# Gated mix of attention and token MLP: the tail of the output projection as half-row products, the o split on GpSimd, and where the max tiles stand

## The chip, the cores and the metric

The kernel runs on one core of one Trainium2 chip. The metric is device time in microseconds of one execution: before the change a median of 1803.75 us over three runs (1803.69 to 1805.62). One execution was profiled; it took 1802.82 us, and its span from the first to the last instruction is 1801.0 us.

The core has five engines with a queue each: TensorE (PE, whose weight loads the profile lists as PEld), VectorE (DVE), ScalarE (ACT), GpSimd (POOL) and SyncE (SP), which here issues all DMAs. Matmuls write to PSUM, of which there are eight banks of 128 x 512 words.

## The reference

`x` is 2048 x 640. Two branches are computed from it and mixed row by row by a gate.

```python
q = (x @ wq).reshape(B, S, 32, 20).transpose(0, 2, 1, 3)   # 32 heads of 20
k, v = x @ wk, x @ wv                                      # one head for all
p = softmax(einsum("bhqd,bkd->bhqk", q, k) * 20 ** -0.5)
a = einsum("bhqk,bkd->bhqd", p, v).transpose(0, 2, 1, 3).reshape(B, S, 640) @ wo
h = layernorm(x)                                           # over the 640 channels
u = gelu(einsum("bsd,sf->bdf", h, w1) + b1)                # over the tokens, F = 1728
b = (einsum("bdf,fs->bds", u, w2) + b2).transpose(0, 2, 1)
out = g * a + (1 - g) * b                                  # g = sigmoid(x . gate_w)
```

Everything is float32.

## The kernel before

**Precision.** A float32 operand is split into a high part, rounded to the type fp32r, and a low part, the rest. A product is then three products in fp32r: high x high, low x high, high x low. The names `oh` and `ol`, `wo_hi` and `wo_lo`, `w2h` and `w2l` are such pairs.

**Units and phases.** Attention is cut into 32 units (`NU`): four heads by 512 queries. A unit has 16 key blocks of 128 keys. The loop at L696 runs over phases `k`, one for each key block of each unit, 513 in all. Phase k issues, in one list for TensorE:

- four score products s (L443, 62 rows by 512 columns), two for key block k - 1 and two for k, all on one half of the rows of TensorE's array: rows 0 to 63 in even phases, 64 to 127 in odd ones (`b = k % 2`). ScalarE takes the exp of each into a tile p (L446);
- four max tiles ms (L284, while there are any): scores of a later unit, whose row maxima VectorE takes (L287) and which later go into the exp's argument;
- up to 16 half-row products with 320 columns of the rest of the work, called fs: first the first MLP layer (L626), then the second (L530), then the output projection (L577). They use the other half of the rows, so that a product of either half can run beside one of the other. They accumulate in the one bank of the pool `ps_g`;
- at the end the four o products of key block k - 1 (L470, `pv_mm`), with 128 rows by 32 columns each.

`beside` (L669) merges two lists, a lane for each row half, by adding up estimated times (`X_US` 0.232 for a product of 512 columns, `F_US` 0.147 for one of 320). In the lane of s there are three max tiles, in the lane of fs one (L702). The order on TensorE and VectorE is the program's own (L695, a manual schedule); ScalarE, GpSimd and SyncE are ordered by the framework's scheduler.

**The flag.** Products on both row halves accumulate in the same bank in turns, one half per phase. So that they don't overlap, `signal` (L454) puts a tiny memset on VectorE behind the last product of a lane, and the first product of the other half (`other_tile`, L449) waits for it.

**How long a phase's list of fs is.** `batches` (L635) spreads the steps of a tile over pairs of phases. First layer: 9 or 10 steps in a phase; second layer: 8 to 11; output projection of row tiles 0 to 11: 7 or 8 up to phase 463, and 15 from 464 to 499 (the long phases). The max tiles end with phase 487; then `spare[0]` is set (L708) and s takes its banks in turns from `ps_m` and `ps_s`, three banks each.

**End of a unit.** After its last o product VectorE transposes the sums (`ot`, L479). The list `later` then holds the steps that follow, one popped in each phase (L710): nothing; `scale` (reciprocal on VectorE L482, multiply on GpSimd L483); `back` (transpose on VectorE, L486); `store` (`oh` on ScalarE L489, `ol` on GpSimd L491, and eight DMAs to the scratch `o_scr`, L495). Once `spare[0]` is set, all four are popped in one phase, and the multiply and `ol` are on VectorE. That concerns units 30 and 31.

**The last four row tiles** (12 to 15) need unit 31, which ends last. From phase 500 (`k_tail`) their o rows of all but the last four heads (560 of 640 rows) are loaded, and phases 502 to 509 compute a part each (a row tile's 320 columns): 15 whole-row products in one bank (L577 through `last_parts`, L722), behind the phase's lanes. VectorE adds the part to the MLP branch (L585) in `spare_row`. After the loop, oh and ol of unit 31 are multiplied with the last four heads' rows of `wo` (L744), added (L745) and stored, one DMA for each row tile.

Of the kernel before, what the change touches and what calls it, by code (L numbers as in the profile page):

```python
# [9 lines left out]
F32 = mybir.dt.float32  # L10
# [27 lines left out]
def mix_kernel(ctx: ExitStack, tc: tile.TileContext, A_x, A_wq, A_wk, A_wv, A_wo,  # L38
# [5 lines left out]
    def f32(ap):  # L44
        return ap.bitcast(F32)
# [390 lines left out]
    def qk(u, pr, b):  # L436
        n, kb = units[u]
        if kb == 4 and pr == 0 and b == 0:
            new_q(n + 1)
        q = qtiles[n]  # L440
        odd_s[0] ^= 1
        s = ps_m.tile([P, NB], F32, name="ms") if spare[0] and odd_s[0] else ps_s.tile([P, NB], F32, name="s")
        nc.tensor.matmul(s, kst[64 * b:64 * b + 62, kb * P:(kb + 1) * P], q[64 * b:64 * b + 62, pr, :],  # L443
                         start=True, stop=True)
        p = pp_pool.tile([P, NB], F32, name="p")
        nc.scalar.activation(p, s, AF.Exp, scale=SCALE)  # L446
        ptiles[u, 2 * pr + b] = p
# [16 lines left out]
    def pv_mm(u):  # L464
        n, kb = units[u]
        if kb == 0:
            otile[0] = ps_o.tile([P, NB], F32, name="o")
        o = otile[0]
        for hh in range(4):
            nc.tensor.matmul(o[32 * hh:32 * hh + 32, :], v_sb[:, kb, :], ptiles.pop((u, hh)),  # L470
                             start=(kb == 0), stop=(kb == NS - 1), skip_group_check=True)
        if kb == NS - 1:
            qb, g = divmod(n, NQ)
            ot = ev.tile([P, NB // 32, 32], F32, name="ot")
            rl = ev.tile([P, NB // 32], F32, name="rl")
            on = ev.tile([P, NB], F32, name="on")
            oh = ev.tile([P, NB], F32R, name="oh")
            ol = ev.tile([P, NB], F32R, name="ol")
            nc.vector.transpose(ot.rearrange("p c e -> p (c e)"), o)  # L479

            def scale():
                nc.vector.reciprocal(rl, ot[:, :, DH])  # L482
                (nc.vector if spare[0] else nc.gpsimd).tensor_mul(ot, ot, rl[:, :, None].to_broadcast([P, NB // 32, 32]))  # L483

            def back():
                nc.vector.transpose(on, ot.rearrange("p c e -> p (c e)"))  # L486

            def store():
                nc.scalar.activation(oh, on, AF.Copy)  # L489
                osplit[:] = [oh, ol]  # L490
                (nc.vector if spare[0] else nc.gpsimd).tensor_sub(ol, on, f32(oh))  # L491
# [53 lines left out]
    def a_jobs(st, part=None):  # L545
        hold = {}
        rows = D if part is None else (H - 4) * DH
        kr = [min(P, rows - c * P) for c in range(DC)]

        def load():  # L550
            oT, yt = oTs[st % 2], yts[st % 2]
            cols = slice(st * P, (st + 1) * P)
            nf = rows // P
            for j in range(2):
                nc.sync.dma_start(out=f32(oT[:, j, :nf]),
                                  in_=o_scr[j, :nf * P, cols].rearrange("(c p) s -> p c s", p=P))
                if nf < DC:
                    nc.sync.dma_start(out=f32(oT[:kr[nf], j, nf]), in_=o_scr[j, nf * P:rows, cols])
            nc.sync.dma_start(out=yt, in_=y_scr[st * P:(st + 1) * P, :])
            hold["o"], hold["y"] = oT, yt  # L560
            if part is None:
                hold["a"] = pools["fin"].tile([P, D], F32, name="yo")
            else:
                hold["a"] = part[st] = spare_row(st)

        halves = [(0, 1) if r > 64 else (0,) for r in kr] if part is None else [(None,)] * DC
        total = 3 * sum(len(h) for h in halves)

        def mm(c, k, d, half):
            if not hold.get("n"):  # L570
                hold["p"], hold["n"] = (ps_m.tile([P, NB], F32, name="ms") if part is not None and d
                                        else ps_g.tile([P, NB], F32, name="g")), 0
# [3 lines left out]
            r = slice(0, kr[c]) if half is None else slice(64 * half, min(kr[c], 64 * half + 64))  # L576
            other_tile(half, nc.tensor.matmul(hold["p"][:, :HD2], o[r, c, :], w[r, c, d * HD2:(d + 1) * HD2],  # L577
                             start=(hold["n"] == 1), stop=(hold["n"] == total)))

        def done(d):  # L580
            sl = slice(d * HD2, (d + 1) * HD2)
            at, yt = hold["a"], hold["y"]
            hold["n"] = 0
            if spare[0]:
                nc.vector.scalar_tensor_tensor(at[:, sl], hold["p"][:, :HD2], g_col[:, st:st + 1], yt[:, sl],  # L585
                                               op0=ALU.mult, op1=ALU.add)
# [3 lines left out]
            if part is None and d == 1:  # L590
                nc.sync.dma_start(out=y_out[st * P:(st + 1) * P, :], in_=at)

        return load, [([[lambda h=h, c=c, k=k, d=d: mm(c, k, d, h) for h in halves[c]]
                        for c in range(DC) for k in range(3)],
                       lambda d=d: done(d)) for d in range(2)]
# [91 lines left out]
    def lane_f(ms, fs):  # L687
        return [(F_US, f) for f in fs] + [(0.0, signal)] + [(X_US, y) for y in ms]

    parts = {}  # L690
    tail = [a_jobs(st, parts) for st in range(NS - 4, NS)]
    last_parts = [(i, p) for i, (load, ps) in enumerate(tail) for p in ps]
    steps, rest = [], []
    w1_upto(4 * PRO + 4)
    with tc.manual_schedule(engines={mybir.EngineType.PE, mybir.EngineType.DVE}):  # L695
        for k in range(len(units) + 1):  # L696
# [2 lines left out]
            if not b:  # L699
                steps, rest = seq[k // 2] if k // 2 < len(seq) else ([], [])  # L700
            fs = [f[1 - b] for f in steps if b or len(f) > 1]
            ms = [[f for f in (ms_next(x) for _ in range(c)) if f] for x, c in ((b, 3), (1 - b, 1))]  # L702
            lanes = [None, None]
            lanes[b] = lane_x(ss, ms[0])
            lanes[1 - b] = lane_f(ms[1], fs)
            beside(*lanes, b)
            ms_done()
            spare[0] = len(row_max) == NU  # L708
            pop_chain()
            for _ in range(4 if spare[0] else 1):  # L710
                f = later.pop(0) if later else None
                if f:
                    f()
            if b:
                for f in rest:
                    f()
            j = k - k_tail
            if j == 0:
                w_last = last_wo()
                tail[0][0]()  # L720
                tail[1][0]()
            if 2 <= j < 2 + len(last_parts):  # L722
                i, (st_steps, done) = last_parts[j - 2]
                for f in st_steps:
                    f[0]()
                done()
                if j % 2 and i + 2 < len(tail):
                    tail[i + 2][0]()
            if k:
                pv_mm(k - 1)  # L730
                n, kb = units[k - 1]
                if kb == 7 and n + 1 < NU:
                    store_max(n + 1)
    for f in later[1:]:
        f()
    oh, ol = osplit
    for i in range(4):
        st = NS - 4 + i
        at = pools["fin"].tile([P, D], F32, name="yo")
        for d in range(2):  # L740
            sl = slice(d * HD2, (d + 1) * HD2)
            acc = ps_m.tile([P, NB], F32, name="ms")
            for k, (o, w) in enumerate(((oh, w_last[0]), (ol, w_last[0]), (oh, w_last[1]))):
                nc.tensor.matmul(acc[:, :HD2], o[:, i * P:(i + 1) * P], w[:, sl], start=(k == 0), stop=(k == 2))  # L744
            nc.vector.scalar_tensor_tensor(at[:, sl], acc[:, :HD2], g_col[:, st:st + 1], parts[st][:, sl],  # L745
                                           op0=ALU.mult, op1=ALU.add)
# [22 lines left out]
```

## Time and profile before

| what | value |
| --- | --- |
| median of three runs | 1803.75 us |
| profiled execution | 1802.82 us, span 1801.0 us |
| mean granted TensorE clock | 0.993 |
| first phase with o products to the last | 215.3 to 1785.7 us |
| long phases with max tiles (464 to 487) | from about 1600 to 1687 us |
| loads and parts of the last four row tiles | about 1737 to 1780 us |
| L446, exp on ScalarE | 1999 x 601 ns on s, 49 more on ms banks |
| L287, reduce on VectorE | 2048 x 683 ns |
| L489, `oh` on ScalarE | 32 x 632 ns; idle before it 22.6 us, for `on` |
| L491, `ol` on GpSimd | 30 x 1274 ns |
| from the last o product's end to the end of the span | 1787.3 to 1801.0 us |

How to read it: the profile gives for each group of instructions the busy time, the mean of one, and the idle time just before them with what ended it. A timeline lists instructions in order of time, merged where they follow each other: start, length, engine, line, operation, output<-input, shape, count, and in brackets the idle time before and its releaser. A row of a window gives, for a stretch of time, the busy time and count of each engine, then the granted clock, the share of the DMA engines and GB/s. An L470 group of eight records is the end of a phase.

### The profile page before, as it was taken

Reading aid. Unit: us, or ns where it says so; the run is one execution under the profiler, and the core shown is the slowest. Engines: PE = TensorE matmul, PEld = TensorE weight load, DVE = VectorE, ACT = ScalarE, POOL = GpSimd, SP = SyncE. Lnnn points to the kernel's source line nnn. Section 1 sums busy time; section 2 is a strip of 40 time slices with the busy share of each in tenths; the row PEclk is TensorE's granted clock in tenths of the full one; section 3 lists DMA queues with packets and bytes.
Section 4 is the critical chain, followed back from the end, with each engine's and each line's share of the span. In section 5 each row is a group of like instructions: output and inputs, shape, how many; then the busy total and the mean of one; then the engine's idle time right before and its main releaser. Section 6 shows DMA issues by size and latency. Waiting matters only on the chain.

```text
span 1801.0 us, 38745 instructions
## 1 busy us (share of the span) xinstructions
PE 1767.1 (98%) x14805; PEld 1141.4 (63%) x14805; DVE 1488.5 (83%) x3052; ACT 1211.6 (67%) x2360; POOL 441.9 (25%) x428
## 2 busy tenths in 40 slices
PE   7989999999999999999999999999999999999998
PEld 5779766666666666566666666666666666566654
DVE  7759999898999898988888888888888888887412
ACT  3334477777777777777777777777777777776653
POOL 6336532323232323142111111111111110111100
PEclk9999999999999999999999999999999999999999
DMA  6555422222222221222211111121111110233321
GB/s 198 158 159 138 106 53 60 66 60 61 66 66 66 66 66 43 73 85 72 65 45 53 58 58 50 54 58 58 58 58 58 48 47 24 63 110 107 98 87 50
DMA packets 155677, 133.66 MB, mean 74 GB/s; under 512 B 18103, under 2 KB 119892, under 8 KB 155492
## 3 DMA queue, kind: packets, MB, share of 16 engines
q1 hardware_dynamic: 155492, 131.18, 25.3%
q8 instruction: 117, 1.92, 0.5%
q14 instruction: 68, 0.56, 0.1%
HBM read 98.50 MB, written 31.13 MB: 72 GB/s over the span
## 4 chain that ended last, share of the span: by engine, by line
PE 91%; DVE 4%; DMA 2%; ACT 1%; issue 1%; POOL 1%; SPq 0%; DVEq 0%; POOLq 0%; ACTq 0%
PE o L470 29%; PE ms L284 17%; PE s L443 17%; PE g L530 11%; PE g L626 7%; PE g L577 4%; PE pp L180 3%; PE pu L391 2%; DVE mp L287 2%; DMA xt<-in_A_x_dram 1%; PE ms L443 1%; PE ms L577 1%; POOL wq_lo L117 0%; POOL slot L156 0%; PE ms L304 0%
## 5 line engine op out<-in xcount | busy, mean ns | idle before, releaser
L287 DVE TENSOR_REDUCE mp<-ms 128x1 f32<-128x512 f32 x2048 | 1279.2, 683 | 172.3 <-PE ms L284 166.4
L446 ACT ACTIVATE p<-s 128x512 f32<-128x512 f32 x1999 | 1047.5, 601 | 366.5 <-PE s L443 351.5
L284 PE MATMUL ms<-kst,qmx 60*128 60x512 f32 x2048 | 848.2, 423 | 4.0 <-DVE mp L287 2.4
L443 PE MATMUL s<-qst,kst 62*128 62x512 f32 x1999 | 745.4, 406 | 1.6 <-issue 1.1
L470 PE MATMUL o<-p,v_sb 128*32 128x512 f32 x4096 | 562.2, 605 | 0.5 <-ACT p L446 0.5
L284 PEld LDWEIGHTS ms<-kst,qmx 60*128 60x128 f32 x2048 | 378.5, 185 | 223.6 <-DVE flag L456 179.4
L443 PEld LDWEIGHTS s<-qst,kst 62*128 62x128 f32 x1999 | 372.1, 186 | 12.6 <-ACT p L446 8.6
L626 PE MATMUL g<-slot,wh 64*128 64x320 f32 x1152 | 282.0, 320 | 0.0
L626 PEld LDWEIGHTS g<-slot,wh 64*128 64x128 f32 x1152 | 191.3, 185 | 54.3 <-DVE flag L456 41.6
L530 PE MATMUL g<-slot,w2h 64*128 64x320 f32 x864 | 214.2, 321 | 0.0
L530 PE MATMUL g<-u,w2h 64*128 64x320 f32 x864 | 214.0, 321 | 0.0
L626 PE MATMUL g<-slot,wl 64*128 64x320 f32 x576 | 180.4, 313 | 0.0
L470 PEld LDWEIGHTS o<-p,v_sb 128*32 128x32 f32 x4096 | 94.4, 108 | 135.3 <-issue 124.1
L530 PEld LDWEIGHTS g<-slot,w2h 64*128 64x128 f32 x864 | 142.8, 184 | 53.7 <-DVE mp L287 28.5
L483 POOL TENSOR_TENSOR ot<-ot,rl 128x512 f32<-128x512 f32 x30 | 31.5, 1050 | 565.9 <-DVE rl L482 563.0
L530 PEld LDWEIGHTS g<-u,w2h 64*128 64x128 f32 x864 | 142.7, 184 | 42.2 <-DVE flag L456 26.8
L338 POOL TENSOR_TENSOR wl<-wr,wh 128x512 fp32r<-128x512 f32 x112 | 149.5, 1339 | 43.9 <-ACT wh L335 36.5
L577 PE MATMUL g<-slot 64*128 64x320 f32 (+1 forms) x780 | 134.1, 319 | 2.5 <-DVE yo L585 2.4
L577 PEld LDWEIGHTS g<-slot 64*128 64x128 f32 (+1 forms) x780 | 116.3, 188 | 28.5 <-DVE flag L456 10.1
L530 PE MATMUL g<-u,w2l 64*128 64x320 f32 x432 | 132.0, 306 | 0.0
L530 PE MATMUL g<-slot,w2l 64*128 64x320 f32 x432 | 132.0, 306 | 0.0
L337 POOL CAST wh<-wr 128x512 fp32r<-128x512 f32 x72 | 44.0, 610 | 293.2 <-PE g L626 293.2
(122 smaller groups left out, 1552.6 us busy)
## 6 DMA issues: line engine op xcount, KB each, us to landing
wr<-in_B_w_dram SPq DMA_DIRECT2D x104, 256.0 KB
qmx<-q_scr SPq DMA_DIRECT2D x192, 80.0 KB
qst<-q_scr SPq DMA_DIRECT2D x192, 80.0 KB
slot<-o_scr SPq DMA_DIRECT2D x24, 320.0 KB
w2r<-in_B_w_dram SPq DMA_DIRECT2D x16, 448.0 KB
w2r<-in_B_w_dram SPq DMA_DIRECT2D x16, 384.0 KB
xt<-in_A_x_dram SPq DMA_DIRECT2D x16, 320.0 KB
q_scr<-qh SPq DMA_DIRECT2D x20, 256.0 KB
```

Of the source, the lines that this page charges most:

```text
L180: nc.tensor.matmul(pp, w[:, c, :], t[c], start=(n == 0), stop=(n == len(pairs) * DC - 1))
L284: nc.tensor.matmul(ms, qmax[n][64 * b:64 * b + 60, pr, qt * P:(qt + 1) * P], kst[64 * b:64 * b + 60, kq * NB:(kq + 1) * NB], start=True, s ...
L287: nc.vector.tensor_reduce(mtiles[n][:, c, kq:kq + 1], ms, axis=AX.X, op=ALU.max)
L337: nc.gpsimd.tensor_copy(wh, wr)
L338: nc.gpsimd.tensor_sub(wl, wr, f32(wh))
L391: nc.tensor.matmul(pu[r][:, :HD2], w[rows, c, :], h[rows, st, :], start=(st == 0 and k == 0), stop=(st == NS - 1 and k == 2))
L443: nc.tensor.matmul(s, kst[64 * b:64 * b + 62, kb * P:(kb + 1) * P], q[64 * b:64 * b + 62, pr, :], start=True, stop=True)
L446: nc.scalar.activation(p, s, AF.Exp, scale=SCALE)
L470: nc.tensor.matmul(o[32 * hh:32 * hh + 32, :], v_sb[:, kb, :], ptiles.pop((u, hh)), start=(kb == 0), stop=(kb == NS - 1), skip_group_check ...
L530: other_tile(half, nc.tensor.matmul(hold["p"][:, :HD2], w[r, fc % FH, :], u[d][r, fc, :], start=(hold["n"] == 1), stop=(hold["n"] == 6 * F ...
L577: other_tile(half, nc.tensor.matmul(hold["p"][:, :HD2], o[r, c, :], w[r, c, d * HD2:(d + 1) * HD2], start=(hold["n"] == 1), stop=(hold["n" ...
L626: other_tile(half, nc.tensor.matmul(hold["p"][:, :HD2], w[r, st % HS, :], h[d][r, st, :], start=(hold["n"] == 1), stop=(hold["n"] == 6 * NS)))
```

## The change

1. **The o split.** `store` becomes two steps, `high` and `low`. `high` takes `oh` on GpSimd, except for the last unit (ScalarE). `low` takes `ol` on GpSimd, except for the last unit (VectorE), and issues the stores. In spare phases two steps are popped instead of four.
2. **Max tiles.** In phases with 12 or more fs, all four max tiles are in the lane of s (`(b, 4), (1 - b, 0)`).
3. **The last parts.** From phase 502 the parts of row tiles 12 to 15 are half-row products in both lanes: `tail_job` makes 30 for rows 0 to 63 and 24 for rows 64 to 127 of each row tile, with an accumulator of its own for each row half and column half (one in `ps_g`, three in `ps_m`), so that no flag is needed. `tail_take` gives them out, 8 or 7 behind the s of one lane and 13 or 16 in the other. VectorE adds each accumulator on its own, four in place of two additions for a row tile. Row tile st + 2 is loaded when st's four are done.
4. **s tiles.** From phase 501 s uses only its own three banks (`not loaded`).
5. **The end.** The output goes through p tiles (twelve buffers) in place of `yo` (two), one DMA for each half row tile.

```diff
-        s = ps_m.tile([P, NB], F32, name="ms") if spare[0] and odd_s[0] else ps_s.tile([P, NB], F32, name="s")
+        s = ps_m.tile([P, NB], F32, name="ms") if spare[0] and odd_s[0] and not loaded else ps_s.tile([P, NB], F32, name="s")
...
-            def store():
-                nc.scalar.activation(oh, on, AF.Copy)
+            def high():
                 osplit[:] = [oh, ol]
-                (nc.vector if spare[0] else nc.gpsimd).tensor_sub(ol, on, f32(oh))
+                if n < NU - 1:
+                    nc.gpsimd.tensor_copy(oh, on)
+                else:
+                    nc.scalar.activation(oh, on, AF.Copy)
+
+            def low():
+                (nc.vector if n == NU - 1 else nc.gpsimd).tensor_sub(ol, on, f32(oh))
                 for j, t in enumerate((oh, ol) if n < NU - 1 else ()):
...
-            later.extend((None, scale, back, store))
+            later.extend((None, scale, back, high, low))
...
+    def tail_load(st):
+        if st < NS:
+            load_a(st, (H - 4) * DH, oTs[st % 2], yts[st % 2])
+            parts[st] = spare_row(st)
+            loaded.append(st)
+
+    def tail_job(st):
+        rows = (H - 4) * DH
+        oT, yt = oTs[st % 2], yts[st % 2]
+        acc, ready = {}, []
+
+        def mm(c, k, d, h, first, last):
+            if first:
+                acc[d, h] = (ps_g.tile([P, NB], F32, name="g") if h and not d
+                             else ps_m.tile([P, NB], F32, name="ms"))
+            o, w = ((oT[:, 0], wo_hi), (oT[:, 1], wo_hi), (oT[:, 0], wo_lo))[k]
+            r = slice(64 * h, min(rows - c * P, 64 * h + 64))
+            nc.tensor.matmul(acc[d, h][:, :HD2], o[r, c, :], w[r, c, d * HD2:(d + 1) * HD2], start=first, stop=last)
+            if last:
+                sl = slice(d * HD2, (d + 1) * HD2)
+                add = parts[st] if d in ready else yt
+                ready.append(d)
+                nc.vector.scalar_tensor_tensor(parts[st][:, sl], acc[d, h][:, :HD2], g_col[:, st:st + 1], add[:, sl],
+                                               op0=ALU.mult, op1=ALU.add)
+                if len(ready) == 4:
+                    tail_load(st + 2)
+
+        for h in range(2):
+            ck = [(c, k) for c in range(DC) if rows - c * P > 64 * h for k in range(3)]
+            for d in range(2):
+                for i, (c, k) in enumerate(ck):
+                    tail[h].append((st, lambda a=(c, k, d, h, i == 0, i == len(ck) - 1): mm(*a)))
+
+    def tail_take(h, n):
+        out = []
+        while len(out) < n and tail[h] and tail[h][0][0] in loaded:
+            out.append(tail[h].pop(0)[1])
+        return out
...
-            ms = [[f for f in (ms_next(x) for _ in range(c)) if f] for x, c in ((b, 3), (1 - b, 1))]
+            ms = [[f for f in (ms_next(x) for _ in range(c)) if f] for x, c in (((b, 3), (1 - b, 1)) if len(fs) < 12 else ((b, 4), (1 - b, 0)))]
             lanes = [None, None]
             lanes[b] = lane_x(ss, ms[0])
+            if k >= k_tail + 2:
+                own = tail_take(b, 7 if b else 8)
+                lanes[b] = [x for i, y in enumerate(lanes[b])
+                            for x in [y] + [(F_US, f) for f in own[2 * i:2 * i + 2]]]
+                fs = tail_take(1 - b, 16 if b else 13)
             lanes[1 - b] = lane_f(ms[1], fs)
...
-            for _ in range(4 if spare[0] else 1):
+            for _ in range(2 if spare[0] else 1):
...
-            j = k - k_tail
-            if j == 0:
+            if k == k_tail:
                 w_last = last_wo()
-                tail[0][0]()
-                tail[1][0]()
-            if 2 <= j < 2 + len(last_parts):
-                i, (st_steps, done) = last_parts[j - 2]
-                for f in st_steps:
-                    f[0]()
-                done()
-                if j % 2 and i + 2 < len(tail):
-                    tail[i + 2][0]()
+                tail_load(NS - 4)
+                tail_load(NS - 3)
...
-        at = pools["fin"].tile([P, D], F32, name="yo")
         for d in range(2):
+            at = pp_pool.tile([P, NB], F32, name="p")
...
-        nc.sync.dma_start(out=y_out[st * P:(st + 1) * P, :], in_=at)
+            nc.sync.dma_start(out=y_out[st * P:(st + 1) * P, sl], in_=at[:, :HD2])
```

`load_a` holds the DMAs that `a_jobs` issued in its `load` before, and `a_jobs` keeps only what the whole row tiles 0 to 11 need.

More of the change, by code (lines that the diff above doesn't have):

```diff
@@ L543, in b2_jobs, with load_a @@
                        lambda d=d: done(d)) for d in range(2)]
-    def a_jobs(st, part=None):
+    def load_a(st, rows, oT, yt):
+        cols = slice(st * P, (st + 1) * P)
+        nf = rows // P
+        for j in range(2):
+            nc.sync.dma_start(out=f32(oT[:, j, :nf]),
+                              in_=o_scr[j, :nf * P, cols].rearrange("(c p) s -> p c s", p=P))
+            if nf < DC:
+                nc.sync.dma_start(out=f32(oT[:rows - nf * P, j, nf]), in_=o_scr[j, nf * P:rows, cols])
+        nc.sync.dma_start(out=yt, in_=y_scr[st * P:(st + 1) * P, :])
@@ new lines, in mix_kernel @@
+    parts = {}
+    tail = [[], []]
+    loaded = []
+    def tail_load(st):
[27 more added lines that the diff above has]
+                    tail[h].append((st, lambda a=(c, k, d, h, i == 0, i == len(ck) - 1): mm(*a)))
@@ L546, in a_jobs @@
+    def tail_take(h, n):
[3 more added lines that the diff above has]
+        return out
+    def a_jobs(st):
         hold = {}
-        rows = D if part is None else (H - 4) * DH
-        kr = [min(P, rows - c * P) for c in range(DC)]
         def load():
             oT, yt = oTs[st % 2], yts[st % 2]
[L552 to L559, printed above, removed]
-            hold["o"], hold["y"] = oT, yt
[L561 to L564, printed above, removed]
@@ L566, in a_jobs @@
-        halves = [(0, 1) if r > 64 else (0,) for r in kr] if part is None else [(None,)] * DC
-        total = 3 * sum(len(h) for h in halves)
+            load_a(st, D, oT, yt)
+            hold["o"], hold["y"] = oT, yt
+            hold["a"] = pools["fin"].tile([P, D], F32, name="yo")
+        total = 6 * DC
         def mm(c, k, d, half):
             if not hold.get("n"):
-                hold["p"], hold["n"] = (ps_m.tile([P, NB], F32, name="ms") if part is not None and d
-                                        else ps_g.tile([P, NB], F32, name="g")), 0
+                hold["p"], hold["n"] = ps_g.tile([P, NB], F32, name="g"), 0
@@ L575, in mm @@
             hold["n"] += 1
-            r = slice(0, kr[c]) if half is None else slice(64 * half, min(kr[c], 64 * half + 64))
+            r = slice(64 * half, 64 * half + 64)
             other_tile(half, nc.tensor.matmul(hold["p"][:, :HD2], o[r, c, :], w[r, c, d * HD2:(d + 1) * HD2],
@@ L589, in done @@
                 nc.gpsimd.tensor_add(at[:, sl], at[:, sl], yt[:, sl])
-            if part is None and d == 1:
+            if d == 1:
                 nc.sync.dma_start(out=y_out[st * P:(st + 1) * P, :], in_=at)
-        return load, [([[lambda h=h, c=c, k=k, d=d: mm(c, k, d, h) for h in halves[c]]
+        return load, [([[lambda h=h, c=c, k=k, d=d: mm(c, k, d, h) for h in range(2)]
                         for c in range(DC) for k in range(3)],
@@ L688, in lane_f @@
         return [(F_US, f) for f in fs] + [(0.0, signal)] + [(X_US, y) for y in ms]
-    parts = {}
-    tail = [a_jobs(st, parts) for st in range(NS - 4, NS)]
-    last_parts = [(i, p) for i, (load, ps) in enumerate(tail) for p in ps]
+    for st in range(NS - 4, NS):
+        tail_job(st)
     steps, rest = [], []
@@ L733, in mix_kernel @@
                     store_max(n + 1)
+    assert not tail[0] and not tail[1]
     for f in later[1:]:
```

2 lines of the change are left out of this document (1 added, 1 removed).

## The prediction

> **What bounds the kernel now.** I read the page first (engines, chain), then TensorE in order of time around single phases, then the waits of the lines the diff touches. A phase is one pass of the loop at L696; it ends with the four o products of L470, so the distance between two starts of L470 is the length of a phase. A unit is 16 phases.
>
> ```profile
> PE 1767.1 (98%) x14805; PEld 1141.4 (63%) x14805; DVE 1488.5 (83%) x3052; ACT 1211.6 (67%) x2360; POOL 441.9 (25%) x428
> PE 91%; DVE 4%; DMA 2%; ACT 1%; issue 1%; POOL 1%; SPq 0%; DVEq 0%; POOLq 0%; ACTq 0%
> ```
>
> TensorE is the bound, and it hardly ever idles. So a gain must come from phases that are longer than their matmuls, which the 98% hides: busy time counts a matmul that is spread out. Four places show it.
>
> ```profile
> 988.10 1.07 PE L470 MATMUL o<-p,v_sb 128*32 128x512 f32 x8
> 991.36 1.11 PE L470 MATMUL o<-p,v_sb 128*32 128x512 f32 x8
> ...
> 1012.40 1.07 PE L470 MATMUL o<-p,v_sb 128*32 128x512 f32 x8
> 1015.28 1.07 PE L470 MATMUL o<-p,v_sb 128*32 128x512 f32 x8
> ```
>
> ```profile
> 986.90 2.06 ACT L446 ACTIVATE p<-s 128x512 f32<-128x512 f32 x4 [1.04 <-PE s L443]
> 989.76 0.63 ACT L489 ACTIVATE oh<-on 128x512 fp32r<-128x512 f32 x1 [0.79 <-DVE on L486]
> 990.30 2.04 ACT L446 ACTIVATE p<-s 128x512 f32<-128x512 f32 x4
> ```
>
> Phase 4 of a unit takes 991.36 - 988.10 = 3.26 us; phase 12 of the same unit, with the same ten mixer products, takes 2.88. In phase 4 ScalarE stands at `oh`, waiting for the transpose `on`, and its four exps come behind it; the o products wait for them.
>
> ```profile
> 1618.74 1.06 PE L470 MATMUL o<-p,v_sb 128*32 128x512 f32 x8
> 1622.36 1.07 PE L470 MATMUL o<-p,v_sb 128*32 128x512 f32 x8
> ...
> 1705.44 1.07 PE L470 MATMUL o<-p,v_sb 128*32 128x512 f32 x8
> 1708.83 1.06 PE L470 MATMUL o<-p,v_sb 128*32 128x512 f32 x8
> ...
> 1749.89 1.07 PE L470 MATMUL o<-p,v_sb 128*32 128x512 f32 x8
> 1754.60 1.07 PE L470 MATMUL o<-p,v_sb 128*32 128x512 f32 x8
> ```
>
> A long phase (15 half-row products) with max tiles takes 3.62 us, one without 3.39, and a phase with a last part of the output projection 4.71.
>
> ```profile
> 1725.06 0.69 DVE L491 TENSOR_TENSOR ol<-on,oh 128x512 fp32r<-128x512 f32 x1 [0.77 <-ACT oh L489]
> 1725.66 0.55 DVE L585 SCALAR_TENSOR_TENSOR yo<-g,g_col,slot 128x320 f32<-128x320 f32 x1
> ...
> 1795.40 1.01 DVE L745 SCALAR_TENSOR_TENSOR yo<-ms,g_col,w2h 128x320 f32<-128x320 f32 x2 [1.00 <-DMA out_dram<-yo]
> ```
>
> ```profile
> 1726.26 0.41 PE L577 MATMUL g<-slot 64*128 64x320 f32 x1 [2.39 <-DVE yo L585]
> ```
>
> ```profile
> 1726.30:1733.00 6.70, 6.70 (x31) 4.71 (x33) 0.06 (x1) 1.73 (x3) 0.00 (x0) 0.52 0.26 63
> ```
>
> At 1723.4 the one g bank waits for `yo`, which stands on VectorE behind the whole o split of unit 30; then, in the row of a window, the granted clock (the 0.52, third from the end) is halved for 6.7 us. At the end VectorE waits 1.00 us for a store.
>
> **A model of a phase** from these rows. A product of 320 columns takes 0.147 us of its lane (starts 144 to 147 ns apart), one of 512 columns 0.23. The longer lane plus 0.19 us, plus 1.0 us of o products: 15 x 0.147 = 2.21, + 0.19 + 1.0 = 3.40 against 3.39 measured; with one max tile more in that lane 3.63 against 3.62. It holds.
>
> **A: the o split on GpSimd.** `oh` leaves ScalarE for 31 of 32 units, and high and low come in two phases. In the changed program TensorE's order is the same up to phase 464, and ScalarE's there has only lost the `oh`. I compared each phase 4 with the median of phases that carry the same products: 0.37 us over it in the 16 units with second-layer products, 0.49 in 11 units with first-layer products, 0.40 in one more; 12.2 us in 28 units. In the long units (3.62) it costs nothing, as ScalarE has room there. All this should go, unless the transpose `on` (0.72 us on VectorE) is what delays the phase; but `ot`, as long and at the same place of the next unit's phase 1, costs 0.01. In first-layer units some gelu steps are held by `on` too (phases of 3.69), so I take 11.5, with 8 and 12.8 (phase 5 gives 0.6 more) as ends. What is added: 31 casts on POOL, 0.61 us each by L337's row. They lie in POOL's idle time (it waits 293 us for TensorE at L337 alone), and `oh` there ends when it ended on ScalarE (0.61 for 0.63). `ol` (1.27) and eight stores follow on SP as before; q loads behind them have over half a unit. Without that cover each unit would pay 0.61, 19 us in all.
>
> The Trainium skill (SBUF — State Buffer, Who interferes with whom) says that a VectorE instruction with two SBUF inputs is blocked by a GpSimd one that reads SBUF, for its whole length. Here the reduces beside POOL's casts keep to 626 to 694 ns, and they read PSUM; by that rule the gelu steps of 11 units could lose 0.61 each, 6.7 us, which would leave A at 4.8.
>
> **B: four max tiles in the lane of s.** It applies to 24 phases (464 to 487; later long phases have no max tiles). The product lane loses 0.232, the other rises to 8 x 0.232 = 1.86, still under 2.21. 24 x (3.62 - 3.39) = 5.5 us. What is new is VectorE's order: four reduces, then the flag that the next phase's first product waits for, where the fourth reduce stood behind the flag. First reduce at 0.5 us into the phase, four in 2.5, flag at 3.1, needed at 3.39: 0.3 us of room. With `ot` in front it is 0.1 late, in one or two phases. Ends: 3 (reduces at 683 ns each and late) and 6.
>
> **C: the stall at 1723.4.** The two phases there take 12.74 us (o at 1722.38 to 1735.11) where 2 x 3.39 = 6.78 is normal: 5.96 lost. After, only rl and the multiply (0.25 + 0.69) stand in front of `yo`: from the flag at 1722.5 that is 0.25 + 0.69 + 0.55 and gaps, 1724.1, against the 1723.4 at which the product is due. 0.7 remain, 5.2 are won, if a gap of 0.7 leaves the clock alone; the 0.45 us gap at 1785 did. Ends 2 and 5.9.
>
> The Trainium skill (TensorE: Matmul & The Clock Gate, Part 1: The HAM clock gate) puts the drop after an idle window of about 3.4 us; here 2.39 us of idling were followed by 0.52, so the trace does not bear out that length. Were the slow clock of another cause, C would be 2.39 - 0.7 = 1.7 and the sum 3.5 smaller.
>
> **D: the last parts in both lanes.** Removed: 120 whole-row products in phases 502 to 509. Added: 216 half-row ones (120 on rows 0 to 63, 96 on the others) in phases 502 to 511. By the model, an even phase has 4 s and 8 products in one lane (0.93 + 1.18 = 2.10) and 13 in the other (1.91): 3.29 us. An odd one has 16 (2.35): 3.54. That pairs of such products run side by side is seen at 152.09 to 152.97, where 12 products of L391 on alternate rows start in 0.88 us, 0.147 a pair. Ten phases: 5 x 3.29 + 5 x 3.54 = 34.2, plus 0.6 for the late o product at 1739.88, which stays. Before, the same ten take 1739.88 to 1782.93 = 43.05. Won: 8.3. ScalarE needs 2.06 us a phase for its exps, so it does not bound them, and s with three banks instead of six is what all phases up to 488 have. The four accumulators keep the two row halves in separate banks, and each buffer is free some 15 products before its next use. The loads: unit 30's stores come about two phases later than now, as `back` waits for phase 498 and low is popped in 499. I place `on` at 3.0 us into 498, oh 0.61 and ol 1.27 on POOL, stores until 0.2 us before phase 500, landed 2 us later (the stores issued until 1728.0 show traffic until 1730.1). The first loads then go out at 1.8 us after 500 begins and the last piece of the first row tile lands about 4.5 after, while phase 502 begins after two phases of 2.65 = 5.3. Room 0.8. Ends: 5 (a load late by 3) and 9.5.
>
> **E: the end.** The 0.69 us low, the transposes and the cast stay. With twelve p tiles for the output the 1.00 us wait at 1795.40 goes, but TensorE at half clock delivers a sum only every 0.8 us, so of it I take 0.8, and 0.1 for a last store of half the size. Ends 0.3 and 1.6.
>
> **Sum.** 11.5 + 5.5 + 5.2 + 8.3 + 0.9 = 31.4. The profiled execution took 1802.82 us (span 1801.0 and 1.8 around it), so 1771.4; the median of the three runs is 0.93 above it, so 1772.4 as a median. All best ends: 35.8, 1768; all worst ends: 18.3, 1785.5.
>
> **Rivals.** (1) A doesn't do what it says: `on` and not `oh` delays phase 4, or the POOL cast comes late. For it: both lie in the same microsecond. Against: `ot` costs nothing. A falls to 2: 1782. (2) The flag takes over: VectorE bounds the 24 long phases at 3.6, and B is 0: 1778. For it: VectorE is 83% busy; against: 0.3 us of room. (3) The last parts don't pair as modelled, or a load is late and the clock halves for 6.7 us (costing 3.2 beside a stall of 3): 1778 to 1782. For it: the room of 0.8 is estimated. (4) Slower: SP and POOL. SP takes its issues in order, and all stores of oh and ol now wait for two POOL steps, with w and q loads behind them; if those loads came after their products, each of 30 units would stall, and from 1.05 us a unit all 31.4 is eaten; at 1.5, 30 x 1.5 - 31.4 = 14 slower, 1817. Against: SP already waits up to 10.0 us for `oh` and TensorE waits for q only 0.6 us in all.
>
> **How the numbers follow.** Forecast 0.64, (1) 0.12, (2) 0.07, (3) 0.12, (4) 0.03, and 0.02 for cases that cancel to nothing. The range 1766.5 to 1784 takes in the forecast and (1) to (3), with 1.5 below the best ends, as some 40 phases are read to 0.04 us; two of the losing cases together fall out. 0.2% is 3.6 us, what a measurement of this kernel can tell from no change: faster 0.95, same 0.02, slower 0.03.
>
> **What would show it.** A: no ACT `oh` before the last, and phase 4 at 2.88 in second-layer units. B: 3.39 between o products from phase 464, and no TensorE wait for the flag. C: a gap of about 0.7 us for `yo` and a granted clock of 1.00 after it. D: ten phases of 3.3 and 3.5, no wait for slot. E: no wait for out_dram. It is wrong if phase 4 stays at 3.2, or if the tail phases exceed 3.8.

## The result, and the profile after

The changed kernel takes 1772.03 us (median of four runs, 1770.2 to 1774.13) against 1803.72 (four runs, 1803.12 to 1805.62). The ratio is 0.9823 with a 95% interval of 0.9806 to 0.9840: 31.7 us less, where the steps summed to 31.4. The profiled execution took 1771.2 us and spans 1769.4.

The page shows the same bound. TensorE is as busy as before, on a shorter span:

```profile
PE 1737.2 (98%) x14901; PEld 1127.8 (64%) x14901; DVE 1487.3 (84%) x3051; ACT 1196.5 (68%) x2329; POOL 461.8 (26%) x460
PE 92%; DVE 3%; DMA 2%; POOL 1%; issue 1%; ACT 0%; SPq 0%; DVEq 0%; POOLq 0%; ACTq 0%
```

The share of 98% moved by nothing while 31.6 us of the span went. This share can't find such time; the distance between o products can. TensorE in order of time, in the unit that the prediction showed (phases 4 and 12):

```profile
980.95 1.06 PE L470 MATMUL o<-p,v_sb 128*32 128x512 f32 x8
983.83 1.07 PE L470 MATMUL o<-p,v_sb 128*32 128x512 f32 x8
...
1004.85 1.06 PE L470 MATMUL o<-p,v_sb 128*32 128x512 f32 x8
1007.73 1.07 PE L470 MATMUL o<-p,v_sb 128*32 128x512 f32 x8
```

Both are 2.88 us long; phase 4 was 3.26. ScalarE and GpSimd there:

```profile
982.71 2.06 ACT L446 ACTIVATE p<-s 128x512 f32<-128x512 f32 x4 [0.90 <-PE s L443]
...
983.94 0.60 POOL L491 CAST oh<-on 128x512 fp32r<-128x512 f32 x1
984.62 1.29 POOL L496 TENSOR_TENSOR ol<-on,oh 128x512 fp32r<-128x512 f32 x1
```

ScalarE has only exps and waits for s alone. The long phases with max tiles, and the phases with last parts:

```profile
1656.31 1.06 PE L470 MATMUL o<-p,v_sb 128*32 128x512 f32 x8
1659.69 1.07 PE L470 MATMUL o<-p,v_sb 128*32 128x512 f32 x8
...
1720.73 1.06 PE L470 MATMUL o<-p,v_sb 128*32 128x512 f32 x8
1724.27 1.06 PE L470 MATMUL o<-p,v_sb 128*32 128x512 f32 x8
```

They take 3.38 (3.62 before) and 3.54 (4.71 before). VectorE at the end of unit 30, VectorE at the very end, and the clock around the end of unit 30 (third from the end in the window's row):

```profile
1705.08 0.69 DVE L483 TENSOR_TENSOR ot<-ot,rl 128x512 f32<-128x512 f32 x1
1705.69 0.54 DVE L629 SCALAR_TENSOR_TENSOR yo<-g,g_col,slot 128x320 f32<-128x320 f32 x1
...
1764.77 1.14 DVE L786 SCALAR_TENSOR_TENSOR p<-ms,g_col,w2l 128x320 f32<-128x320 f32 x2 [0.25 <-PE ms L785]
```

```profile
1700.00:1710.00 10.00, 9.89 (x76) 6.48 (x76) 2.88 (x8) 6.06 (x12) 1.07 (x2) 1.00 0.21 64
```

`yo` comes right behind the multiply, and the clock stays whole. At the end VectorE waits for TensorE's sums, no longer for a store.

**Where the time went, phase by phase.** The table adds up distances between starts of L470; the end runs from the last such start to the end of the span. Every run below has the same three blind spots: the time of the first o products, which moved between 214.1 and 218.0 us from run to run with no edit near it, phases 2 to 19 (52.7 to 54.1), and the end. The second is phase 2 and the clock: in e7, e10 and e12 phase 2 is 1.0 to 1.3 us longer than in the changed kernel, and there a stretch of 6.8 us at a granted clock of 0.50 outlasts the first o products by 2.2 to 2.9 us. In the other runs the stretch at 0.50 just before them is 3.4 us long (e6 has none) and ends at most 0.5 us after they start. All other phases repeat to some hundredths of a microsecond where their code is the same, so one profile of a kernel is enough to price an edit there.

| kernel | phases 20-463 | 464-487 | 488-497 | 498-499 | 500-512 | end | span |
| --- | --- | --- | --- | --- | --- | --- | --- |
| before | 1332.56 | 87.05 | 34.71 | 12.73 | 50.57 | 15.35 | 1801.0 |
| changed | 1320.17 | 81.63 | 34.82 | 7.38 | 41.85 | 15.51 | 1769.4 |
| e1, `oh` on ScalarE | 1332.52 | 81.62 | 34.55 | 7.38 | 41.85 | 14.55 | 1780.7 |
| e2, split in one step | 1320.01 | 81.61 | 34.82 | 7.38 | 41.87 | 14.47 | 1767.1 |
| e3, max tiles 3 and 1 | 1320.03 | 87.05 | 34.74 | 7.39 | 41.85 | 14.87 | 1775.1 |
| e4, whole-row parts | 1320.01 | 81.62 | 34.83 | 7.38 | 54.69 | 14.16 | 1780.2 |
| e5, before, two pops | 1332.80 | 87.05 | 34.71 | 7.39 | 50.56 | 15.52 | 1798.9 |
| e6, before, cast on GpSimd | 1320.07 | 87.05 | 34.74 | 11.22 | 50.60 | 15.54 | 1786.0 |
| e7, old end | 1320.00 | 81.59 | 34.83 | 7.38 | 41.85 | 16.34 | 1770.2 |
| e8, idle products at the end | 1320.28 | 81.62 | 34.82 | 7.38 | 41.85 | 13.23 | 1766.8 |
| e9, whole rows, six s banks | 1320.19 | 81.62 | 34.83 | 7.38 | 50.57 | 14.88 | 1778.7 |
| e10, the cast three times | 1323.34 | 81.60 | 34.82 | 7.38 | 42.75 | 14.71 | 1774.2 |
| e11, both lanes from 488 | 1320.00 | 81.62 | 28.88 | 5.63 | 41.90 | 14.92 | 1760.1 |
| e12, e11 and three edits | 1319.99 | 81.62 | 28.86 | 5.64 | 42.54 | 12.87 | 1759.9 |

### The profile page after: what moved, and what is told of

Its sections match the earlier page's. It is cut to its first block, busy times and chain, and to the rows that moved or that the text cites. A ratio compares the mean times of both kernels' runs of the same rounds, so it can differ in the third digit from the quotient of the medians.

```text
span 1769.4 us, 38903 instructions
## 1 busy us (share of the span) xinstructions
PE 1737.2 (98%) x14901; PEld 1127.8 (64%) x14901; DVE 1487.3 (84%) x3051; ACT 1196.5 (68%) x2329; POOL 461.8 (26%) x460
## 4 chain that ended last, share of the span: by engine, by line
PE 92%; DVE 3%; DMA 2%; POOL 1%; issue 1%; ACT 0%; SPq 0%; DVEq 0%; POOLq 0%; ACTq 0%
PE o L470 29%; PE ms L284 17%; PE s L443 17%; PE g L535 11%; PE g L670 7%; PE g L621 4%; PE pp L180 3%; PE pu L391 2%; DVE mp L287 2%; DMA xt<-in_A_x_dram 1%; PE ms L581 1%; POOL slot L156 0%; DMA ht<-in_A_wq_dram 0%; PE ms L304 0%; PE ms L785 0%
## 5 line engine op out<-in xcount | busy, mean ns | idle before, releaser
L446 ACT ACTIVATE p<-s 128x512 f32<-128x512 f32 x2022 | 1059.5, 601 | 393.0 <-PE s L443 378.5
L470 PE MATMUL o<-p,v_sb 128*32 128x512 f32 x4096 | 558.5, 605 | 0.5 <-ACT p L446 0.5
L443 PEld LDWEIGHTS s<-qst,kst 62*128 62x128 f32 x2022 | 375.9, 186 | 11.2 <-issue 7.2
L470 PEld LDWEIGHTS o<-p,v_sb 128*32 128x32 f32 x4096 | 92.7, 108 | 132.6 <-issue 123.6
L621 PE MATMUL g<-slot 64*128 64x320 f32 x720 | 121.3, 314 | 0.1
L621 PEld LDWEIGHTS g<-slot 64*128 64x128 f32 x720 | 105.5, 184 | 23.1 <-DVE flag L456 18.4
```

## The experiments

e1 to e10 are one profiled execution each; e11 and e12 are four executions each, one of them profiled.

**e1: is it the engine?**

```diff
-                if n < NU - 1:
-                    nc.gpsimd.tensor_copy(oh, on)
-                else:
-                    nc.scalar.activation(oh, on, AF.Copy)
+                nc.scalar.activation(oh, on, AF.Copy)
```

> The changed kernel with the cast `oh` back on ScalarE for all units; it keeps its own step, `ol` stays on GpSimd one phase later. Theory (the cast's place in ScalarE's queue, ahead of four exps, is what lengthens phase 4): phase 4 of the units with second-layer products goes back from 2.88 to 3.26 us, those of the 28 units sum to about 12 us over phases with the same products, and the span grows from 1769.4 to about 1781. Rival (two steps in place of one are what helped): phase 4 stays at 2.88 to 2.95, the span within 2 us of 1769.4.

Phases 20 to 463 go back by 12.35 us, from 1320.17 to 1332.52; in before they were 1332.56. TensorE and ScalarE in order of time, phase 4 of the same unit:

```profile
988.22 1.06 PE L470 MATMUL o<-p,v_sb 128*32 128x512 f32 x8
991.48 1.10 PE L470 MATMUL o<-p,v_sb 128*32 128x512 f32 x8
```

```profile
989.88 0.63 ACT L490 ACTIVATE oh<-on 128x512 fp32r<-128x512 f32 x1 [0.79 <-DVE on L486]
990.42 2.04 ACT L446 ACTIVATE p<-s 128x512 f32<-128x512 f32 x4
```

3.26 us again, with the cast in front of the exps again. The transpose `on` is the same instruction in both kernels, so it is not what lengthens phase 4. The rival falls.

**e2: is it the two steps?**

```diff
-            later.extend((None, scale, back, high, low))
+            later.extend((None, scale, back, lambda: (high(), low())))
```

> The changed kernel with `oh` and `ol` both on GpSimd, but popped in one step, so that a unit's split ends a phase earlier in the program. Theory (only the engine counts): phase 4 stays at 2.88 in second-layer units, the span within 1.5 us of 1769.4. Rival (the two steps carry the gain, or part of it): phase 4 or 5 grows by 0.1 to 0.4 us in each of 28 units, 3 to 11 us in all.

Phases 20 to 463 take 1320.01 us, no phase after them differs by more than 0.03, and the span is 2.4 us shorter only through the blind spots (the first o products 1.1 earlier, the end 1.0 shorter). The engine carries A; the second step gives nothing. The expectation on the span was missed by 0.9, the one on the phases was met.

**e3: the max tiles.**

```diff
-            ms = [... for x, c in (((b, 3), (1 - b, 1)) if len(fs) < 12 else ((b, 4), (1 - b, 0)))]
+            ms = [... for x, c in ((b, 3), (1 - b, 1))]
```

> The changed kernel with three max tiles in the lane of s and one in the other lane in all phases, as before the change. Theory (the longer lane sets a long phase): phases 464 to 487 take 3.62 instead of 3.39 us, the span grows by 5.4 us to about 1774.8. Rival (VectorE's order around the flag bounds the long phases in either form): they stay within 0.1 us of 3.39, the span within 2 us of 1769.4.

Phases 464 to 487 take 87.05 us, to the hundredth what they took before: 5.42 us for 24 phases, 0.226 each. The longer lane sets them, and the flag behind the fourth reduce does not show.

**e4 and e9: the last parts.** e4 puts the parts back as whole-row products behind the lanes; e9 also gives s both pools to the end.

```diff
-                own = tail_take(b, 7 if b else 8)
-                lanes[b] = [x for i, y in enumerate(lanes[b])
-                            for x in [y] + [(F_US, f) for f in own[2 * i:2 * i + 2]]]
-                fs = tail_take(1 - b, 16 if b else 13)
+                fs = []
...
             beside(*lanes, b)
+            if k >= k_tail + 2:
+                for f in tail_take(0, 1):    # one whole-row part of 15 products
+                    f()
...
-        s = ps_m.tile(...) if spare[0] and odd_s[0] and not loaded else ps_s.tile(...)    # e9 only
+        s = ps_m.tile(...) if spare[0] and odd_s[0] else ps_s.tile(...)
```

> The changed kernel with the last parts as 15 whole-row products in one bank behind the lanes of phases 502 to 509, as before the change; o split, max tiles and the end stay. Theory (the pairing of row halves carries D): phases 502 to 509 take 4.7 us, 510 and 511 about 2.2 to 2.7; from the o products of phase 501 to those of 511 43 us instead of 34.4, the span grows by 8 to 9 us to about 1778. Rival (the s tiles' banks or the loads made the gain): phases 502 to 509 take under 4.2 us, the span grows by less than 5.

Phases 502 to 509 took 5.19 to 5.25 us, more than the 4.7 expected, and the span grew by 10.8. TensorE of e4 in order of time:

```profile
1717.69 0.96 PE L443 MATMUL s<-qst,kst 62*128 62x512 f32 x3
1718.88 0.50 PE L443 MATMUL s<-qst,kst 62*128 62x512 f32 x1 [0.23 <-ACT p L446]
```

Three s go at once, the fourth waits until ScalarE has read the first bank. So this run carried a cost of its own, and by itself does not price the pairing.

> As the run with whole-row last parts, but s again takes its banks in turns from both pools (six instead of three) to the end, which is the tail as it was before the change. Theory (that run lost 0.54 us a phase to four s in a row on three banks, and the rest is the pairing): phases 502 to 509 take 4.71 us, phases 500 to 511 together 47.8 against 39.7 of the changed kernel and 52.5 of that run. Rival (something else of the new tail lengthened those phases): they stay at 5.2.

With six banks the phases are 4.71 and the stretch 500 to 512 is 50.57 us, as before. The step from e9 to the changed kernel, 8.72 us, is the pairing with its banks; three banks under four s in a row cost 0.54 a phase. In the lanes, with products between one s and the next, phases 502 to 511 keep to the model of the prediction, which has no such cost; phase 501, without products, loses 0.55 (3.14 for 2.59), and phase 512 is shorter by about as much (2.18 for 2.76).

**e5: the stall alone.** In the kernel before:

```diff
-            for _ in range(4 if spare[0] else 1):
+            for _ in range(2 if spare[0] else 1):
```

> The kernel before, with one edit: two steps of `later` popped per phase instead of four once the max tiles have ended; `oh` and `ol` stay on ScalarE and VectorE in one step. Theory (C: `yo` stood on VectorE behind the whole split, and the idle time brought the clock down): phases 498 and 499 together fall from 12.74 to about 7.4 us, the granted clock stays at 1.00 there, span 1801.0 to about 1796. Rival (the drop of the clock has another cause): the wait shrinks by 1.7 us, but a window of some 6 us with a clock near 0.5 stays, span about 1799.

The two phases fall from 12.73 to 7.39 us. The span hardly shows it: the first o products came 2.7 us later in this run. The window in which the clock was halved before:

```profile
1726.00:1733.00 7.00, 6.89 (x58) 4.89 (x54) 2.52 (x7) 5.09 (x10) 0.00 (x0) 1.00 0.08 19
```

Without the idle time the clock stays at 1.00, with `oh` still on ScalarE and `ol` on VectorE. So it was the idle time that brought the clock down, and C is worth 5.34 us through the order on VectorE alone.

**e6: the cast alone.** In the kernel before, in one step with `ol`, for the units before the max tiles end:

```diff
-                nc.scalar.activation(oh, on, AF.Copy)
+                if spare[0]:
+                    nc.scalar.activation(oh, on, AF.Copy)
+                else:
+                    nc.gpsimd.tensor_copy(oh, on)
```

> The kernel before, with one edit: `oh` on GpSimd in place of ScalarE in the 30 units before the max tiles end, in the same single step as `ol`. Theory (A is the engine alone and adds up with the rest): phase 4 falls from 3.26 to 2.88 in second-layer units, span 1801.0 to about 1789 (12 less). Rival (the gain needs the step of its own, or `on` on VectorE delays phase 4): span within 4 us of 1801.

Phases 20 to 463 lose 12.49 us and fall to 1320.07. A adds up with the rest and needs none of it. One thing moved that was not touched: phases 498 and 499 took 11.22 us in place of 12.73, with the same order on VectorE. VectorE and TensorE at the stall, and the window of the slow clock:

```profile
1711.37 0.69 DVE L494 TENSOR_TENSOR ol<-on,oh 128x512 fp32r<-128x512 f32 x1 [0.84 <-ACT oh L490]
1711.98 0.54 DVE L588 SCALAR_TENSOR_TENSOR yo<-g,g_col,slot 128x320 f32<-128x320 f32 x1
```

```profile
1712.58 0.41 PE L580 MATMUL g<-slot 64*128 64x320 f32 x1 [2.39 <-DVE yo L588]
```

```profile
1713.90:1717.30 3.40, 3.40 (x17) 1.73 (x15) 0.06 (x1) 1.03 (x2) 0.00 (x0) 0.51 0.31 81
```

TensorE idled for the same 2.39 us, but the slow clock that followed lasted 3.4 us in place of the 6.7 in before, and so the same stall lost 1.5 us less. A stall of this kind has no fixed price.

**e7 and e8: the end.** e7 takes `yo` tiles and one store for each row tile, as before. e8 keeps TensorE at work while it waits for `oh`:

```diff
+        idle = ps_s.tile([P, NB], F32, name="s")
+        for i in range(14):
+            nc.tensor.matmul(idle, kst[:62, :P], qtiles[NU - 1][:62, 0, :], start=True, stop=True)
     assert not tail[0] and not tail[1]
```

> The changed kernel with the end as before: `yo` tiles (two buffers) and one store for each row tile. From the start of the last o products to the end of the span the kernel before took 15.35 us, the changed one 15.49. Theory (TensorE at half clock bounds the end, so the buffers change little): 15.2 to 16.3 us, with half clock until about 6 us after the first last product; the wait for a store shows only if the clock comes back early. Rival (half-width stores are the slow part of the new end): 14.5 or less.

> The changed kernel with 14 idle products of 512 columns into a free bank after the last o products (about 3.0 us, read by nobody), in the 3.3 us in which TensorE waits for `oh`. Theory (the end is bounded by the halved clock): granted clock 1.00 through the last 24 products, which then take about 3.4 us of TensorE and are bounded by VectorE's eight additions of 0.55 (4.4 us); from the start of the last o products to the end 13.5 to 14.2 us instead of 15.49. Rival (VectorE or the stores bound the end): within 0.4 us of 15.49.

e7's end took 16.34 us, just above its range, and there the store did show:

```profile
1764.59 1.01 DVE L786 SCALAR_TENSOR_TENSOR yo<-ms,g_col,w2h 128x320 f32<-128x320 f32 x2 [2.10 <-DMA out_dram<-yo]
```

With the three other runs that have the old end (15.35, 15.52, 15.54) the mean is 15.69; eight runs with the new end took 14.16 to 15.51, mean 14.76. The new end is 0.9 us shorter on average, but single pairs say anything from -0.2 to 2.2. e8's end took 13.23. TensorE and VectorE of e8, and the clock:

```profile
1755.08 3.53 PE L776 MATMUL s<-qst,kst 62*128 62x512 f32 x14
...
1758.54 0.71 PE L788 MATMUL ms<-w2h,oh 128*128 128x320 f32 x3
```

```profile
1759.79 1.01 DVE L789 SCALAR_TENSOR_TENSOR p<-ms,g_col,w2h 128x320 f32<-128x320 f32 x2 [0.65 <-PE ms L788]
1760.71 1.00 DVE L789 SCALAR_TENSOR_TENSOR p<-ms,g_col,w2l 128x320 f32<-128x320 f32 x2
```

```profile
1755.50:1762.00 6.50, 6.44 (x33) 5.03 (x32) 4.97 (x10) 0.63 (x1) 0.00 (x0) 1.00 0.11 39
```

With the clock kept, VectorE's additions follow each other without a gap: it, and no longer TensorE, bounds the end. The theory held, and the end came out 0.3 shorter than its range.

**e10: how much room has GpSimd?** The cast is made three times.

```diff
-                    nc.gpsimd.tensor_copy(oh, on)
+                    for _ in range(3):
+                        nc.gpsimd.tensor_copy(oh, on)
```

> The changed kernel with the cast `oh` on GpSimd made three times over in each of 31 units (same values), 1.2 us of GpSimd more per unit. Theory (GpSimd's part of the split is hidden and the DMA queue behind it has room): phase 4 stays at 2.88 in second-layer units, phases 20 to 463 within 0.5 us of 1320.2, and only the stores of unit 30 come 1.2 us later, which may cost phase 502 up to 0.5. Rival (GpSimd or the queue sits close to the path): each unit pays, 28 x 0.3 to 1.2, phases 20 to 463 at 1328 or more.

Phase 4 stays at 2.88, but phases 20 to 463 take 3.2 us more: the theory's 0.5 was wrong, and so was the rival's 8. It is not spread over the units: phase 5 is 0.62 to 0.97 longer than in the changed kernel in four of them (units 3, 6, 8 and 11, all with first-layer products) and the same in the others. VectorE and GpSimd of e10 in order of time, in the first of the four:

```profile
368.70 1.45 DVE L365 SCALAR_TENSOR_TENSOR slot<-t,slot 128x320 fp32r<-128x320 f32 x1
```

```profile
366.46 1.97 POOL L492 CAST oh<-on 128x512 fp32r<-128x512 f32 x3 [2.30 <-DVE on L486]
368.51 1.29 POOL L497 TENSOR_TENSOR ol<-on,oh 128x512 fp32r<-128x512 f32 x1
```

The same step in the changed kernel:

```profile
367.20 0.48 DVE L365 SCALAR_TENSOR_TENSOR slot<-t,slot 128x320 fp32r<-128x320 f32 x1
```

A gelu step of VectorE with two inputs in SBUF stands behind GpSimd's subtraction, to its end (368.51 + 1.29 = 369.80, and 370.15 = 369.80 + 0.35 for the step's own end). In the changed kernel `ol` ends at 366.93, before the step begins at 367.20. So the late GpSimd work cost through VectorE, not through the DMA queue. At the other end the stores of unit 30 came late: phase 502 took 4.24 us instead of 3.35, with a wait of 0.62 for the loads.

**e11 and e12: a better version.** The lanes are unequal in the other long phases too: without max tiles 0.93 us of s stand beside 2.21 of products. e11 gives row tiles 9 to 11 to `tail_job` as well.

```diff
-    aj = [a_jobs(st) for st in range(NS - 4)]
+    aj = [a_jobs(st) for st in range(NS - 7)]
...
-            if k >= k_tail + 2:
-                own = tail_take(b, 7 if b else 8)
+            early = k_tail - 12 <= k < k_tail
+            if early or k >= k_tail + 2:
+                own = tail_take(b, 4 if early else 7 if b else 8)
...
-                fs = tail_take(1 - b, 16 if b else 13)
+                fs = tail_take(1 - b, 11 if early else 16 if b else 13)
```

> The changed kernel with row tiles 9 to 11 in both lanes as well (phases 488 to 499: 4 products behind s in one lane, 11 in the other, an accumulator for each row half), and s on three banks from there on. Theory (the longer lane sets a phase): 11 x 0.147 + 0.19 + 1.0 = 2.81 us instead of 3.39, 12 phases save 7.0, and the excess of phases 488, 490 and 498 (0.5, 0.25, 0.6) goes in part; against it the loads of the last row tiles have 1.7 us less time and may cost phase 502 about 1. Span phases from the first o products to the last shorter by 6 to 8, median about 1765. Rival (ScalarE's exps or the loads bound these phases): 3.2 us or more a phase, or the saving returns as a wait at phase 502.

Phases 490 to 496 and 499 take 2.80 to 2.81 us where 2.81 was worked out (488, 489, 497 and 498 take 3.29, 3.01, 2.96 and 2.84), and phases 488 to 499 together 34.51 instead of 42.20: 7.7 less. Phase 502 stays at 3.39. The median is 1763.62 us (four runs, 1761.86 to 1765.54) against 1802.67 before on that chip, a ratio of 0.9790 (0.9772 to 0.9808).

e12 adds e8's idle products, unit 30's multiply on GpSimd, and both pools for s in phase 501.

> As the run before with row tiles 9 to 11 in both lanes, and three more edits: idle products behind the last o products keep the clock up, unit 30's multiply is on GpSimd, and s has both pools in phase 501. Theory: 7 from the lanes, 1.5 from the end (13.2 us instead of 14.7 on average), up to 0.6 in phase 498 and 0.5 in 501: median 1761 to 1764. Rival (the edits compete for the same waits): no better than the run with the lanes alone.

1763.16 us (1761.69 to 1763.55), ratio 0.9783 (0.9768 to 0.9797); the intervals overlap, so it is not told apart from e11. Two of its parts are seen in the profile: the end is 12.87 instead of 14.92, and phase 501 2.16 instead of 2.72. The multiply gave nothing in phase 498 (2.85 for 2.84), where up to 0.6 was expected. And phase 502 is 4.59 instead of 3.39 and waits for the loads of the first row tile. What phase 501 gave was lost there, with more; in that part the rival holds.

## Why the prediction was right

The sum was right, and so were A to D, each seen alone in the table; E failed in the profiled pair. That 31.4 lies so near to the measured 31.6 of the spans is in part luck: A gave 0.9 more than forecast and D 0.4 more, E 1.1 less.

- **A**: 11.5 forecast; 12.39 in the profiled pair, 12.35 by undoing it (e1), 12.49 by doing it alone (e6). Phase 4 alone gave 11.35, so the 11.5 was right for it, with its deduction for gelu steps: phase 4 keeps some 0.8 of its excess, most of it in first-layer units. The other 1.04 came from other phases (0.44 from phase 5), which the forecast had only in its best end. The three excesses by kind of unit multiply out to 11.7 and not to 12.2, since 0.49 is the common value of the 11 units and units 3 and 8 have 0.8. The first rival is refuted by e1, and e2 shows that the two steps are not part of the gain.
- **The rule named beside A.** By the Trainium skill (SBUF — State Buffer, Who interferes with whom) the gelu steps could have lost up to 6.7 us to the cast. The changed kernel shows no loss there: the GpSimd work ends 0.27 us before the step of e10's example begins. e10 shows the rule at work: 1.45 us for a step of 0.48. The prediction's reading of it, a price if the two meet, was right; with a single cast they did not meet.
- **B**: 5.5 forecast, 5.42 measured, and 5.42 back by undoing it (e3). VectorE's flag did not come into it.
- **C**: 5.2 forecast, 5.35 in the pair, 5.34 alone (e5). Phase 498 keeps 0.61 of excess, where 0.7 was forecast. That the idle time makes the slow clock is shown by e5. The Trainium skill (TensorE: Matmul & The Clock Gate, Part 1: The HAM clock gate) asks for an idle window of about 3.4 us; 2.39 us were enough here, and by that length C would have been 3.5 smaller.
- **D**: 8.3 forecast, 8.72 over phases 500 to 512, and 8.72 by undoing it (e9). Even phases took 3.32 to 3.35 for a modelled 3.29, odd ones 3.53 to 3.55 for 3.54. The 0.6 of the late o product did not stay at 502; phase 501 became 0.55 longer instead, which goes with the three s banks (3.13 in e4, 2.59 in e9). The room of the loads, 0.8 by the prediction, was nearer 0.5: in e10 unit 30's casts took 1.35 us longer (1.96 for 0.61), and phase 502 lost 0.89.
- **E**: 0.9 forecast, and in the profiled pair the end was 0.16 longer. The wait for the store went, as forecast (1.00 us before, 2.10 with the old end in e7). What failed for that pair is the clock: at the end it was 0.50 for 3.4 us before and for 6.8 us after (windows of the two profiles, in this order):

```profile
1791.40:1794.80 3.40, 3.40 (x14) 3.40 (x14) 2.19 (x4) 0.00 (x0) 0.00 (x0) 0.50 0.25 95
1758.10:1764.90 6.80, 6.13 (x23) 6.13 (x24) 4.09 (x8) 0.61 (x1) 0.00 (x0) 0.50 0.17 54
```

Over twelve runs the two ends differ by the 0.9 forecast. The four with the old end all have 3.4 us of half clock there (mean 15.69). Of the new ones five have 3.4 (e1 to e4 and e10, mean 14.55) and three have 6.8 (changed, e9 and e11, mean 15.10). At the same clock the edit is worth about 1.1, by these means, though three of the four old ends ran on a chip on which the new one was not run as it is. The right estimate would have been a range around 0.9, and the timed median can't show it.

The second rival (the flag) and the third (no pairing) are refuted by e3 and by the phases of D. The fourth, slower through GpSimd and the DMA queue, was not seen at the load of the change; tripling the cast cost 3.2 us through another path and 0.9 through the stores, far from 31.

## What to carry to other kernels

Where one engine is busy nearly all the time, measure a repeating mark (here the o products) and compare periods that hold the same work: the excess of single periods is where a gain can be had, and it can be added up beforehand. Model a stretch with two lanes as its longer lane plus fixed parts; level the lanes first. An instruction that waits must not stand in front of work that the bound engine needs next, on whatever engine it waits, and one late addition can cost more through the clock than through its own time.

## What the runs showed of the hardware

- A VectorE step with two SBUF inputs took 1.45 us instead of 0.48 while GpSimd ran a subtraction (e10); reduces from PSUM beside the o split took a median of 0.68 us in the changed kernel, as without it.
- After 2.39 us without a matmul the granted clock was 0.52 for 6.7 us (before); after the same 2.39 us in e6 it was 0.51 for 3.4 us. The end shows the same two lengths, 3.4 and 6.8 us. After a gap of 0.62 (e10, phase 502) it stayed at 1.00. Idle products through a wait of 3.3 us kept it at 1.00 (e8).
- The first o products started between 214.1 and 218.0 us in runs with the same code before them, while 444 phases behind them repeated within 0.3 us in sum.
